# A Fourier-mixing kernel on one core: the last block of the hidden DFT matrix and its mirrors fetched by one gather of 128 half rows, blocks counted from row 1

## The chip, the cores and the metric

The kernel runs on one core of one Trainium2 chip. The metric is the device time of one execution in microseconds. Three executions of the kernel before took 199.15, 200.08 and 200.59 us; the median, 200.08 us, is its time.

## The reference

The input `x` has 2048 tokens of 576 numbers. The reference normalises each token, transforms the result with a discrete Fourier transform along the hidden dimension and one along the sequence, keeps the real part and adds the input:

```
a = einsum("bsd,ed->bse", ln(x), dft_hid_re);  b = einsum("bsd,ed->bse", ln(x), dft_hid_im)
y = einsum("ts,bse->bte", dft_seq_re, a) - einsum("ts,bse->bte", dft_seq_im, b)
h = x + y
r = ln(h) @ w_r;  idx = argmax(r)                  # one token of 2048
f = (silu(ln(h)[idx] @ w_gate) * (ln(h)[idx] @ w_up)) @ w_down      # 576 -> 4608 -> 576
out = h + ln(h);  out[idx] += f * sigmoid(r[idx])
```

The DFT matrices are inputs: the kernel must compute with what it is given, whatever it holds. Two of 2048x2048 (here `ct`, cosine and sine in turn) and two of 576x576 (here `wt`: row e holds the 576 real parts and then the 576 imaginary parts, 4608 bytes in all).

## The kernel before

**The folds and their checks.** A DFT matrix is symmetric to itself mirrored: of `wt`, row 576-e has the real part of row e and the negative of its imaginary part, and the same holds of the columns. So the kernel multiplies by half of the rows and columns and gets the other half by sums and differences. It may do so only if the matrices that it was given have these symmetries, so it checks them on the way: it loads a block and its mirror, VectorE (DVE) writes their difference into a buffer `Q` (two halves, used in turn), and ScalarE (ACT) squares that with an accumulated sum (L368) into a column of `DS`. Near the end the sums are tested; a sum that is too large sends the kernel into a generic branch. Checks of `ct` are DVE lines L375 (a half against its mirror), L380 (a block against another) and L387; those of `wt` are `off_w` (L422 to L427).

**W.** The hidden DFT matrix lies in tile `W` as three blocks: A holds rows 0 to 127, B rows 128 to 255, C rows 256 to 288. In C the real parts lie on partitions 0 to 32, and the imaginary parts of rows 256 to 287 a second time on partitions 64 to 95, so that one matmul can take both. `load_w` issues these loads on the queue of the sync engine (SP): L403 for A, B and for C's 33 rows, L405 for the 32 half rows. The mirrored rows of A, B and C are fetched row by row on GpSimd's (POOL's) queue by indirect DMAs (`gather`, L301) with row numbers from the columns of `iw`; they land in buffers of the ring R or in D and exist only for the check. `wrap_w` (ACT, L415) copies column 0 behind column 575. The matmuls with W (the hidden transform, L610) come in five steps: A and B with their real parts, with their imaginary parts, and C.

**Stages.** (1) Tokens are loaded, folded and normalised (to about 33 us); XF holds the folded tokens. (2) Sequence transform (PE, L565): halves of `ct` in two groups, `GROUPS`, each a cosine and a sine half, loaded from SP (L357) and, mirrored, gathered from POOL (L301), into the tiles D and the seven buffers of the ring R. DVE and ACT combine the results into `Z` (L579, L583). (3) Hidden transform (L610, 58.7 to 126 us), the residual sum on DVE (L619), the router's dot product (L623, L630). (4) The router's argmax, the chosen token, and the feed-forward of that token: 4608 columns of `w_gate` and `w_up` and rows of `w_down`, 31.85 MB, are loaded into places that the earlier stages leave free (R, D, XF, W, Z, Q; L1181). Their products with the token are made on POOL (L1209), DVE (L1198) and PE (L1236), their sums on ACT (L1214). (5) The last PE products (`pd`), a sum `orow` (L1249), the output.

**The order.** A planner (class `Plan`) is given every step with an engine, an estimated duration and its predecessors, and writes out each engine's order by list scheduling. It also hands out buffers (`ring`, for R and D; `qs`, for Q), and picks the order and the places of the feed-forward's weights. Every engine executes its order strictly in turn, with semaphore waits at single instructions. The wish list for stage 2 is a string: `"sffsffwsss"`, where `s` is the check of a sine block of the second group, `f` a first step of a cosine block, and `w` the check of W (`w_check`: three gathers and three `off_w`).

Of the kernel before, what the change touches and what calls it, by code (L numbers as in the profile page):

```python
# [142 lines left out]
def kernel(  # L143
# [265 lines left out]

# [3 lines left out]
    def wrap_w(n):  # L413

        act.activation(W[n][:, :, D : D + 1], W[n][:, :, 0:1], AF.Copy)  # L415

    def off_w(n, u):

        ps = W_ROWS[n]
        t, o = WM["ABC"[n]][0:ps], Q[0:ps, u % 2]  # L420
        re, im = W["ABC"[n]][0:ps, 0, :], W["ABC"[n]][0:ps, 1, :]
        dve.tensor_tensor(o[:, 0:D], t[:, 0:D], re[:, 0:D], op=OP.subtract)  # L422
# [1 line left out]
        o = o[:, 2 * D : 3 * D]
        dve.tensor_tensor(o[:, 0:287], re[:, 1:HD], re[:, D - 1 : HD : -1], op=OP.subtract)
        dve.tensor_tensor(o[:, 287:575], im[:, 1 : HD + 1], im[:, D - 1 : HD - 1 : -1], op=OP.add)
        dve.tensor_copy(o[:, 575:576], im[:, 0:1])  # L427

    W_ROWS = (P, P, 33)

# [108 lines left out]
    def folded(k, part):  # L539
        n = POS[k]  # L540
        q = FOLDED.index(k)
        e, o = FO[k] if k in PAIRS else (UF[k][:, 1:289], UF[k][:, 289:D])
        b = BE[:, n : n + 1] if k in PAIRS else BX[:, n : n + 1]
        sc = 1.0 if k in PAIRS else RX[:, n : n + 1]
        if part == 0:
            act.activation(XF[:, q, E0 + 1 : E0 + 289], e[:, :288], AF.Identity, bias=b, scale=sc)
        else:
            dve.tensor_scalar(XF[:, q, O0 + 1 : O0 + 288], o[:, :287], sc, None, op0=OP.mult)

# [138 lines left out]

    dve.memset(XF[:, :, 289 : O0 + 1], 0.0)
    dve.memset(XF[:, :, O0 + 288 : XF_W], 0.0)  # L690
    dve.memset(W["C"], 0.0)

# [170 lines left out]

    WS, WL, WRAP = [], [], []

    def w_first():
        for n in range(3):
            LAST["SP"], d = load(
                "SP", then(load_w, None, n), (0.59, 0.59, 0.22)[n], LAST["SP"], users["W" + "ABC"[n]]
            )  # L870
            WL.append(d)

    def w_check():
        for n in range(3):
# [87 lines left out]
    for j in GROUPS[0][:3]:
        c_check(j, 0)
    w_first()
    for j in GROUPS[0][3:]:
# [546 lines left out]
```

## Time and profile before

| | us |
|---|---|
| median of 3 runs | 200.08 (199.15 to 200.59) |
| profiled execution | 199.06 |
| its span | 197.1 |
| DVE busy | 166.4 (84%) |
| ACT busy | 140.5 (71%) |
| PE busy | 130.2 (66%) |
| POOL busy | 111.8 (57%) |
| moved by DMA | 77.81 MB, mean 395 GB/s |

The profiled execution took 2 us more than its span, which starts with its first and ends with its last recorded instruction. Times in a timeline count from the start of the span. A row of a timeline has the start, the duration, the engine, the line, the operation, the tile written `<-` the tiles read, and in square brackets how long the engine had stood idle before and what released it. A row of the windows has, for each engine, its busy time in that stretch (with the count of instructions), then the granted clock of TensorE, the mean busy share of the 16 DMA engines (which can come out above 1, as packets overlap) and the GB/s that they moved. "SPq" is SP's queue: its waits are those of the loads that it issues.

### The profile page before, as it was taken

How to read it: one execution, taken by the hardware profiler on the slowest of the kernel's cores; microseconds unless marked ns; L12 is line 12 of the kernel's file. 1: busy time of each engine (PE TensorE's matmuls, PEld its weight loads, DVE VectorE, ACT ScalarE, POOL GpSimd, SP SyncE). 2: the span in 40 equal slices, each digit the busy share in tenths (PEclk: the TensorE clock that was granted, in tenths of full speed). 3: DMA queues.
4: the chain of work that ended last, by engine and by line, in shares of the span. 5: the costliest groups of instructions: out<-in, count | busy, mean ns of one | idle time of the engine just before them, and what ended most of it. 6: DMA issues, size and time to landing. Idle time of an engine off the chain costs nothing. (4 is left out here: it accounts for less than half of the span.)

```text
span 197.1 us, 2789 instructions
## 1 busy us (share of the span) xinstructions
PE 130.2 (66%) x758; PEld 89.5 (45%) x758; DVE 166.4 (84%) x419; ACT 140.5 (71%) x259; POOL 111.8 (57%) x134
## 2 busy tenths in 40 slices
PE   0007889999999999999999986700241317074940
PEld 0004667755667788676866764400121103032330
DVE  4399999989899699995999999999839999987620
ACT  3298865781997879797588599989527999787600
POOL 6588888724447882398830000004556999999700
PEclk9999999999999999999999999985555555567596
DMA  5999999999999999999999999999999999999980
GB/s 183 422 412 413 409 415 406 411 394 326 401 406 396 406 379 410 409 406 415 407 408 416 422 425 419 428 421 409 430 429 417 432 423 425 423 424 421 419 354 24
DMA packets 14491, 77.81 MB, mean 395 GB/s; under 512 B 1855, under 2 KB 1859, under 8 KB 11143
## 3 DMA queue, kind: packets, MB, share of 16 engines
q1 hardware_dynamic: 10461, 56.56, 71.1%
q0 software_dynamic: 4000, 21.03, 26.5%
q8 instruction: 7, 0.11, 0.2%
q14 instruction: 13, 0.11, 0.1%
q10 hardware_dynamic: 10, 0.00, 0.0%
HBM read 72.86 MB, written 6.49 MB: 403 GB/s over the span
## 5 line engine op out<-in xcount | busy, mean ns | idle before, releaser
L368 ACT ACTIVATE Q<-Q 128x2944 bf16<-128x2944 bf16 (+5 forms) x26 | 55.4, 2132 | 15.7 <-DVE Q L380 8.2
L610 PE MATMUL py<-W,Z 128*128 128x289 f32 x180 | 45.3, 409 | 2.5 <-DVE X L619 2.5
L565 PE MATMUL ps<-D,XF 128*128 128x320 f32 (+3 forms) x216 | 44.8, 408 | 0.4 <-DMA D<-in_ct_dram 0.4
L610 PEld LDWEIGHTS py<-W,Z 128*128 128x128 f32 x180 | 33.6, 189 | 13.9 <-issue 2.2
L301 POOL DMA_INDIRECT R<-in_ct_dram,ic x21 | 29.3, 1396 | 18.0 <-DVE Q L375 14.1
L565 PEld LDWEIGHTS ps<-D,XF 128*128 128x128 f32 (+1 forms) x216 | 32.1, 172 | 12.8 <-issue 2.4
L1209 POOL TENSOR_TENSOR D<-D,Z 128x1152 f32<-128x1152 f32 x8 | 20.9, 2640 | 0.0
L667 POOL DMA_DIRECT2D out_dram<-X x1 | 0.6, 606 | 33.5 <-ACT X L661 33.5
L301 POOL DMA_INDIRECT D<-in_ct_dram,ic x11 | 14.8, 1346 | 7.6 <-DMA R<-in_ct_dram,ic 4.6
L498 ACT ACTIVATE junk<-X,XT 128x576 bf16<-128x576 f32 x16 | 12.3, 772 | 7.6 <-DVE W L459 6.4
L1214 ACT ACTIVATE junk<-D 128x576 bf16<-128x576 f32 x20 | 13.7, 683 | 3.2 <-POOL D L1209 1.6
L375 DVE TENSOR_TENSOR Q<-R,D 128x896 bf16<-128x896 f32 x11 | 11.9, 1084 | 3.9 <-DMA D<-in_ct_dram 2.4
L1236 PE MATMUL pd<-XF,H 128*1 128x144 f32 x80 | 5.3, 438 | 14.8 <-DVE H L1228 11.3
L537 PE MATMUL fo<-W,diag 128*128 128x288 f32 (+1 forms) x8 | 3.7, 640 | 16.0 <-DVE diag L528 16.0
L380 DVE TENSOR_TENSOR Q<-R,D 128x1152 bf16<-128x1152 f32 x10 | 13.4, 1348 | 0.0
L630 ACT ACTIVATE junk<-X,TD 128x576 bf16<-128x576 f32 x16 | 12.3, 766 | 1.4 <-DVE X L619 1.3
L661 ACT ACTIVATE X<-X,BB,UP 128x576 f32<-128x576 f32 x14 | 10.8, 854 | 3.1 <-DVE BB L642 3.1
L387 DVE TENSOR_TENSOR Q<-D 128x640 bf16<-128x640 f32 (+3 forms) x20 | 12.8, 694 | 0.0
L623 DVE SCALAR_TENSOR_TENSOR junk<-X,wr 128x576 bf16<-128x576 f32 x16 | 12.1, 755 | 0.3
L375 DVE TENSOR_TENSOR Q<-D 128x896 bf16<-128x896 f32 x11 | 11.8, 1082 | 0.0
L619 DVE SCALAR_TENSOR_TENSOR X<-py,X 128x576 f32<-128x576 f32 x16 | 11.6, 748 | 0.0
L375 DVE TENSOR_TENSOR Q<-R 128x896 bf16<-128x896 f32 x10 | 10.7, 1083 | 0.2 <-DMA R<-in_ct_dram,ic 0.2
(202 smaller groups left out, 257.5 us busy)
## 6 DMA issues: line engine op xcount, KB each, us to landing
D<-in_ct_dram SPq DMA_DIRECT2D x22, 576.0 KB
R<-in_ct_dram SPq DMA_DIRECT2D x10, 576.0 KB
D<-in_wu_dram SPq DMA_DIRECT2D x5, 1152.0 KB
D<-in_wd_dram SPq DMA_DIRECT2D x4, 1152.0 KB
R<-in_wg_dram SPq DMA_DIRECT2D x3, 1152.0 KB
D<-in_wg_dram SPq DMA_DIRECT2D x3, 1152.0 KB
out_dram<-X SPq DMA_DIRECT2D x2, 1440.0 KB
X<-in_x_dram SPq DMA_DIRECT2D x4, 576.0 KB
```

What stands on the lines that cost most here:

```text
L301: pool.indirect_dma_start(tile, None, view, bass.IndirectOffsetOnAxis(ap=rows, axis=0), element_offset=at)
L368: act.activation(t, t, AF.Square, accum_out=DS[0 : t.shape[0], n : n + 1])
L375: dve.tensor_tensor(o, C[j, i, True][:, 0:7, :], C[j, i, False][:, 7:0:-1, :], op=SIGN[i])
L380: dve.tensor_tensor(o, C[NK - j, i, False], C[j, i, False][:, :, ::-1], op=SIGN[i])
L387: dve.tensor_tensor(o[:, :, k::2, :], t[:, :, k::2, 0:HM], t[:, :, k::2, HM:P], op=op)
L498: act.activation(junk[:, 0:D], X[:, k, 0:D], AF.Square, bias=XT[:, n : n + 1], scale=-float(D), accum_out=VX[:, n : n + 1],)
L565: pe.matmul(cm(ZP[g, n][k % 2][p0 : p0 + m], w), XF[:, q, m0 : m0 + m], DT[g, i][:, :, k, 0:HM], start=k in (0, 1), stop=k in (6, 7),)
L610: pe.matmul(YP[GROUPS[g][c]][:, h, 0:w], Z[:, a, c * P : (c + 1) * P], w_block(a)[:, h * HD : h * HD + w], start=(a == 0), stop=(a == 4),)
L623: dve.scalar_tensor_tensor(junk2, X[:, k, 0:D], 1.0, wr, op0=OP.mult, op1=OP.mult, accum_out=TD[:, n, 0:1])
L630: act.activation(junk[:, 0:D], X[:, k, 0:D], AF.Square, bias=TD[:, n, 1:2], scale=-float(D), accum_out=VAR[:, n : n + 1],)
L1209: pool.tensor_tensor(t, t, xs.unsqueeze(1).to_broadcast([P, JW, D]), op=OP.mult)
L1214: act.activation(junk[:, 0:D], WB[w, j][:, r, :], AF.Copy, accum_out=acc[:, j + r : j + r + 1])
```

## The change

Blocks of W now start at row 1: A holds rows 1 to 128, B rows 129 to 256, and C rows 257 to 288. C is no longer loaded from SP: one gather on POOL's queue fetches 128 half rows of 2304 bytes (`wh`, `wt` seen as 1152 half rows). Partitions 0 to 31 get the real parts of rows 257 to 288, 32 to 63 those of the mirror rows 319 down to 289 and of row 0, and 64 to 127 the imaginary parts likewise (with row 288 once more in the last lane). Two half rows, the imaginary parts of rows 0 and 288, come from SP into partitions 0 and 1 behind it. So C brings its mirrors along, and `w_check` gathers mirrors for A and B only.

The half rows' numbers stand in column 2 of `iw`. They are made by a new function, `last_block_rows`: four IOTAs of 32 rows, and for the lane of row 0 a comparison, a cast, a product and a write back. This and the gather form the step `wc_first`, which is planned with the loads of W, ahead of the fourth check of the first group.

C's check, `off_wc`, writes 865 columns on 128 partitions rather than 1728 on 33: a clearing of 576 columns of Q, two differences of 31 rows, a copy of the two half rows and the column check on 64 rows (`off_e`); ACT squares 865 columns on 128 rows. The clearing of tile C at the start (L691, DVE) is gone, since the gather fills every partition. The wish list is now `"sffsffswcss"`: the mirrors of A and B are gathered and checked behind one more sine check, and `c` is C's check. The columns of XF are laid out to fit (E1 = 0, the column of row 0 at 319, O1 = 320).

```diff
@@ E0, O0, XF_W
-E0, O0, XF_W = 0, 320, 640
+E1, E_0, O1, XF_W = 0, 319, 320, 640
+D1 = 2 * P + 1
@@ index tables
+    wh = wt.rearrange("d (c e) -> (d c) e", c=2)
...
-        pool.iota(iw, pattern=[[-P, 3]], base=D, channel_multiplier=-1)
-        pool.memset(iw[0:1, 0:1], 0)
+        pool.iota(iw[:, 0:2], pattern=[[-P, 2]], base=D - 1, channel_multiplier=-1)
...
+    def last_block_rows():
+        for c in range(2):
+            p = 64 * c
+            pool.iota(iw[p : p + 32, 2:3], pattern=[[0, 1]], base=2 * D1 + c, channel_multiplier=2)
+            pool.iota(iw[p + 32 : p + 64, 2:3], pattern=[[0, 1]], base=2 * (D - D1) + c, channel_multiplier=-2)
+        r, f = iw[32:64, 2:3], [small.tile([P, 1], F32, tag=f"rw{n}", name=f"rw{n}", bufs=1)[32:64] for n in range(2)]
+        pool.tensor_scalar(f[0], r, D + 0.5, None, op0=OP.is_ge)
+        pool.tensor_copy(f[1], r)
+        pool.tensor_tensor(f[0], f[0], f[1], op=OP.mult)
+        pool.tensor_scalar(r, f[0], 1.0, 0.0, op0=OP.mult, op1=OP.add)
@@ load_w
-        name = "ABC"[n % 3]
-        if n < 3:
-            t = W[name][:, :, 0:D]
-            rows = wt[n * P : n * P + (P if n < 2 else 33), :].rearrange("p (c e) -> p c e", c=2)
-            sp.dma_start(t if n < 2 else t[0:33], rows)
-            if n == 2:
-                sp.dma_start(W[name][64:96, 0, 0:D], wt[2 * P : HD, D : 2 * D])
-            return
-        t = WM[name] = raw(b, f"w{name}m").rearrange("p a e -> p (a e)")
-        gather(t if n < 5 else t[0:33, :], wt, iw[:, n - 3 : n - 2] if n < 5 else iw[0:33, 2:3])
+        if n < 2:
+            rows = wt[n * P + 1 : (n + 1) * P + 1, :].rearrange("p (c e) -> p c e", c=2)
+            sp.dma_start(W["AB"[n]][:, :, 0:D], rows)
+        elif n == 2:
+            sp.dma_start(W["C"][0:2, 1, 0:D], wh[1 : D + 2 : D, :])
+        elif n < 5:
+            name = "AB"[n - 3]
+            t = WM[name] = raw(b, f"w{name}m").rearrange("p a e -> p (a e)")
+            gather(t, wt, iw[:, n - 3 : n - 2])
+        else:
+            gather(W["C"][:, 0, 0:D], wh, iw[:, 2:3])
@@ checks
+    def off_wc(u):
+        c, o = W["C"][:, 0, :], Q[:, u % 2, 0 : D + 289]
+        dve.memset(o[:, 0:D], 0.0)
+        for p, op in ((0, OP.subtract), (64, OP.add)):
+            dve.tensor_tensor(o[p : p + 31, 0:D], c[p + 32 : p + 63, 0:D], c[p : p + 31, 0:D], op=op)
+        dve.tensor_copy(o[32:34, 0:D], W["C"][0:2, 1, 0:D])
+        off_e(o[:, D:], c[0:64], c[64:P])
@@ plan
+    def wc_first():
+        r = LAST["POOL"] = add("POOL", 1.5, last_block_rows, LAST["POOL"])
+        LAST["POOL"], d = load("POOL", then(load_w, None, 5), 0.295, r)
+        WC.append(d)
...
+    def wc_check():
+        q, w = qs.take()
+        WS.append(add("DVE", 2.6, then(off_wc, q), WL[2], WC, w))
+        squares(q, D + 289, WS[-1])
...
-    for step in "sffsffwsss":
+    for step in "sffsffswcss":
```

What the planner makes of it is seen in the order of three engines. On POOL, the first rows are the gathers of mirrored halves of `ct` into R and D around 32 to 40 us of the profile before:

```order
L521 TENSOR_TENSOR XF<-V_111 128x2
L301 DMA R<-in_ct_dram,ic 128x896
L301 DMA D<-in_ct_dram,ic 128x896 x2
L301 DMA R<-in_ct_dram,ic 128x896 x7
L301 DMA R<-in_wt_dram,iw 128x1152
L301 DMA D<-in_wt_dram,iw 128x1152
L301 DMA D<-in_wt_dram,iw 33x1152
```

The same place now, with the semaphores that each instruction waits for (those whose names begin with DMASW are raised by the landing of POOL's own DMAs; `rw` are the two small tiles of `last_block_rows`):

```order
L315 DMA R<-in_ct_dram,ic 128x896
L315 DMA D<-in_ct_dram,ic 128x896 [waits PE_49]
L235 IOTA iw 32x1
L236 IOTA iw 32x1 [waits Pool_49]
L235 IOTA iw 32x1
L236 IOTA iw 32x1 [waits Pool_49]
L238 TENSOR_SCALAR rw_403<-iw 32x1 [waits DMASW5_49,DMASW4_49,DMASW6_49,DMASW1_49,DMASW7_49,DMASW0_49,Pool_49]
L239 CAST rw_404<-iw 32x1
L240 TENSOR_TENSOR rw_403<-rw_403,rw_404 32x1 [waits Pool_49]
L241 TENSOR_SCALAR iw<-rw_403 32x1 [waits Pool_49]
L315 DMA W<-in_wt_dram,iw 128x576 [waits Pool_49]
L315 DMA D<-in_ct_dram,ic 128x896 [waits PE_49]
```

Eight small instructions and C's gather have moved in between the two gathers into D; the first of the four that reshape the numbers waits for six of POOL's DMA semaphores. Behind the last row stand eight gathers into R, one into D and the two of W's mirrors.

On SP, the loads of the halves of `ct` and of W, before:

```order
L357 DMA D<-in_ct_dram 128x1152 x10
L357 DMA R<-in_ct_dram 128x1152 x2
L357 DMA D<-in_ct_dram 128x1152
L403 DMA W<-in_wt_dram 128x2x576 x2
L403 DMA W<-in_wt_dram 33x2x576
L405 DMA W<-in_wt_dram 32x576
L357 DMA D<-in_ct_dram 128x1152
```

and now:

```order
L371 DMA D<-in_ct_dram 128x1152 x10
L371 DMA R<-in_ct_dram 128x1152 x2
L371 DMA D<-in_ct_dram 128x1152
L415 DMA W<-in_wt_dram 128x2x576 x2
L417 DMA W<-in_wt_dram 2x576
L371 DMA D<-in_ct_dram 128x1152
```

Two narrow loads have become one of two half rows at the same place. Further down SP's order, the first of the feed-forward's weights goes into XF, where before it went into R.

On DVE, the checks of C and what stands around them, before (`py` is a result of the hidden transform, `TD` the router's dot products):

```order
L427 CAST Q<-W 128x1
L422 TENSOR_TENSOR Q<-D,W 33x576
L423 TENSOR_TENSOR Q<-D,W 33x576
L425 TENSOR_TENSOR Q<-W 33x287
L426 TENSOR_TENSOR Q<-W 33x288
L427 CAST Q<-W 33x1
L619 SCALAR_TENSOR_TENSOR X,TD<-py_1_551,X 128x576
```

and now:

```order
L446 CAST Q<-W 128x1
L451 MEMSET Q 128x288
L453 TENSOR_TENSOR Q<-W 31x576 x2
L454 CAST Q<-W 2x576
L443 TENSOR_TENSOR Q<-W 64x287
L445 TENSOR_TENSOR Q<-W 64x288
L446 CAST Q<-W 64x1
L649 SCALAR_TENSOR_TENSOR junk_124,TD<-X,wr 128x576
```

Seven instructions stand where five stood, and they read no mirror buffer. The first check of W, which before stood ahead of the first two residual sums (L619), now stands behind them and three more checks of `ct`.

More of the change, by code (lines that the diff above doesn't have):

```diff
@@ L232, in unit_matrix @@
         dve.scalar_tensor_tensor(
-            sgn, ident[:, D // 2 - 2 * P : D // 2 - 2 * P + 1], -0.5, pm1, op0=OP.mult, op1=OP.add
+            sgn, ident[:, HD - D1 : HD - D1 + 1], -0.5, pm1, op0=OP.mult, op1=OP.add
         )
@@ L413, in wrap_w, with off_e @@
     def wrap_w(n):
-        act.activation(W[n][:, :, D : D + 1], W[n][:, :, 0:1], AF.Copy)
+        c = 1 if n == "C" else 2
+        act.activation(W[n][:, 0:c, D : D + 1], W[n][:, 0:c, 0:1], AF.Copy)
     def off_w(n, u):
-        ps = W_ROWS[n]
-        t, o = WM["ABC"[n]][0:ps], Q[0:ps, u % 2]
-        re, im = W["ABC"[n]][0:ps, 0, :], W["ABC"[n]][0:ps, 1, :]
+        t, o = WM["AB"[n]], Q[:, u % 2]
+        re, im = W["AB"[n]][:, 0, :], W["AB"[n]][:, 1, :]
         dve.tensor_tensor(o[:, 0:D], t[:, 0:D], re[:, 0:D], op=OP.subtract)
         dve.tensor_tensor(o[:, D : 2 * D], t[:, D : 2 * D], im[:, 0:D], op=OP.add)
[L424 to L429, printed above, removed]
+        off_e(o[:, 2 * D : 3 * D], re, im)
+    def off_e(o, re, im):
+        h = o.shape[-1] - 289 if re.shape[0] == P else 0
+        dve.tensor_tensor(o[0 : re.shape[0], 0:287], re[:, 1:HD], re[:, D - 1 : HD : -1], op=OP.subtract)
+        o = o[:, h:] if h else o[64:P]
+        dve.tensor_tensor(o[:, 0:288], im[:, 1 : HD + 1], im[:, D - 1 : HD - 1 : -1], op=OP.add)
+        dve.tensor_copy(o[:, 288:289], im[:, 0:1])
+    def off_wc(u):
[5 more added lines that the diff above has]
+        off_e(o[:, D:], c[0:64], c[64:P])
     VX = mp.tile([P, NK], F32, name="VX")
@@ L514, in biases @@
         q = FOLDED.index(ORDER[n0])
-        d0 = XF[:, q : q + (h if n0 < 14 else 2), E0]
+        d0 = XF[:, q : q + (h if n0 < 14 else 2), E_0]
         if n0 == 14:
@@ L545, in folded @@
         if part == 0:
[L546 removed]
+            act.activation(XF[:, q, E1 : E1 + 288], e[:, :288], AF.Identity, bias=b, scale=sc)
         else:
[L548 removed]
+            dve.tensor_scalar(XF[:, q, O1 : O1 + 287], o[:, :287], sc, None, op0=OP.mult)
     ZP = {}
@@ L559, in seq @@
         ZP[g, n] = [zbank(f"ps{g}_{n}_{h}") for h in range(2)]
-        parts = [(0, E0 + 2 * P, 64, 0), (1, O0 + 2 * P, 64, 64)]
+        parts = [(0, E1 + 2 * P, 64, 0), (1, O1 + 2 * P, 64, 64)]
         if n < 4:
-            parts = [(n // 2, (E0, O0)[n // 2] + (n % 2) * P, P, 0)]
+            parts = [(n // 2, (E1, O1)[n // 2] + (n % 2) * P, P, 0)]
         for q, k in enumerate(FOLDED):
@@ L687, in then @@
         return lambda: f(*args)
-    dve.memset(XF[:, :, 289 : O0 + 1], 0.0)
-    dve.memset(XF[:, :, O0 + 288 : XF_W], 0.0)
-    dve.memset(W["C"], 0.0)
+    dve.memset(XF[:, :, E1 + 288 : E_0], 0.0)
+    dve.memset(XF[:, :, O1 + 287 : XF_W], 0.0)
     moved = [add("DMA", 1.5, None)]
@@ L862, in c_check @@
         squares(u, QW if j in PAIRS else 7 * P, n)
-    WS, WL, WRAP = [], [], []
+    WS, WL, WRAP, WC = [], [], [], []
     def w_first():
@@ L868, in w_first @@
             LAST["SP"], d = load(
-                "SP", then(load_w, None, n), (0.59, 0.59, 0.22)[n], LAST["SP"], users["W" + "ABC"[n]]
+                "SP", then(load_w, None, n), (0.59, 0.59, 0.005)[n], LAST["SP"], users["W" + "ABC"[n]]
             )
             WL.append(d)
+    def wc_first():
+        r = LAST["POOL"] = add("POOL", 1.5, last_block_rows, LAST["POOL"])
+        LAST["POOL"], d = load("POOL", then(load_w, None, 5), 0.295, r)
+        WC.append(d)
     def w_check():
-        for n in range(3):
-            u, d = ring("POOL", load_w, (0.59, 0.59, 0.16)[n], n + 3)
+        for n in range(2):
+            u, d = ring("POOL", load_w, 0.59, n + 3)
             q, w = qs.take()
@@ L961 @@
         c_half(0, c, m)
[L962 to L965, printed above, removed]
+    for n, j in enumerate(GROUPS[0]):
+        if n == 3:
+            w_first()
+        if n == 3:
+            wc_first()
         c_check(j, 0)
@@ L976 @@
     for n in range(3):
-        WRAP.append(add("ACT", 0.25, then(wrap_w, "ABC"[n]), WL[n], SEQ[0, 2][0]))
+        WRAP.append(add("ACT", 0.25, then(wrap_w, "ABC"[n]), WL[n] if n < 2 else WC, SEQ[0, 2][0]))
     no_more("D2")
@@ L985 @@
             c_first(1, 0, (next(first),))
+        elif step == "c":
+            wc_check()
         else:
```

2 lines of the change are left out of this document (1 added, 1 removed).

## The prediction

> **What bounds the kernel now.** I read the page first (busy shares, the slices of DMA, the chain), then the last rows of PE and POOL, then DVE's waits going back, and last the stretch of DMA in which W's last block is loaded.
>
> Busy shares of the engines, and DMA in 40 slices of 4.9 us:
>
> ```profile
> PE 130.2 (66%) x758; PEld 89.5 (45%) x758; DVE 166.4 (84%) x419; ACT 140.5 (71%) x259; POOL 111.8 (57%) x134
> DMA  5999999999999999999999999999999999999980
> GB/s 183 422 412 413 409 415 406 411 394 326 401 406 396 406 379 410 409 406 415 407 408 416 422 425 419 428 421 409 430 429 417 432 423 425 423 424 421 419 354 24
> ```
>
> The transfers are busy from 4.9 us to about 190 at some 410 to 430 GB/s. No engine is as full. The end, on PE, and the start and the last row of POOL's products:
>
> ```profile
> 188.02 1.16 PE L1236 MATMUL pd<-D,H 128*1 128x144 f32 x32 [0.74 <-DVE hs L1227]
> 190.11 1.16 PE L1236 MATMUL pd<-W,H 128*1 128x144 f32 x32 [0.93 <-SPq L1339]
> 149.47 2.62 POOL L1209 TENSOR_TENSOR XF<-XF,Z 128x1152 f32<-128x1152 f32 x1 [2.96 <-ACT Z L1084]
> 183.09 2.64 POOL L1209 TENSOR_TENSOR D<-D,Z 128x1152 f32<-128x1152 f32 x1
> ```
>
> The last product waits 0.93 us for its weights, so the end is DMA's. Right behind stands a chain of compute: POOL's products, one after another from 149.47 to 185.73, and their sums. If all transfers came earlier, the end would come earlier by 0.93 us, and by more only if 149.47 does so too. That start hangs on the chosen token, hence on DVE. Its waits in the stages that the change touches:
>
> ```profile
> 42.88 1.09 DVE L375 TENSOR_TENSOR Q<-R,D 128x896 bf16<-128x896 f32 x1 [0.52 <-ACT Q L368]
> 52.18 1.09 DVE L375 TENSOR_TENSOR Q<-R,D 128x896 bf16<-128x896 f32 x1 [0.95 <-ACT Q L368]
> 66.17 1.09 DVE L375 TENSOR_TENSOR Q<-R 128x896 bf16<-128x896 f32 x1 [0.22 <-DMA R<-in_ct_dram,ic]
> 69.07 0.76 DVE L422 TENSOR_TENSOR Q<-R,W 128x576 bf16<-128x576 f32 x1 [1.80 <-DMA R<-in_wt_dram,iw]
> 93.52 1.09 DVE L375 TENSOR_TENSOR Q<-R,D 128x896 bf16<-128x896 f32 x1 [2.41 <-DMA D<-in_ct_dram]
> ```
>
> Up to 60 us DVE waits for ACT alone; later it waits for DMA, 0.22 + 1.80 + 2.41 = 4.43 us in all. So before 60 DVE and ACT set the pace, and after it DMA does. On this the sum rests.
>
> **C's narrow loads.** Two loads on SP bring C, 148.5 and 72 KB, onto 33 and 32 partitions. When they move, DMA dips (windows of 1 and 2 us; the last two columns are DMA's busy share and GB/s):
>
> ```profile
> 44.00:45.00 1.00, 1.00 (x10) 0.57 (x8) 1.00 (x1) 0.31 (x1) 0.00 (x0) 1.00 1.09 423
> 45.00:46.00 1.00, 1.00 (x12) 0.50 (x9) 1.00 (x2) 0.00 (x0) 0.00 (x0) 1.00 0.97 348
> 46.00:47.00 1.00, 1.00 (x10) 0.51 (x8) 1.00 (x2) 0.00 (x0) 0.49 (x1) 1.00 1.11 266
> 47.00:48.00 1.00, 1.00 (x7) 0.44 (x4) 1.00 (x4) 0.16 (x1) 1.00 (x1) 1.00 1.02 281
> 48.00:49.00 1.00, 1.00 (x5) 0.74 (x4) 1.00 (x2) 0.37 (x1) 0.70 (x2) 1.00 1.02 318
> 49.00:50.00 1.00, 1.00 (x5) 0.68 (x5) 1.00 (x2) 0.60 (x1) 1.00 (x1) 1.00 1.01 358
> 58.00:59.00 1.00, 1.00 (x5) 0.55 (x4) 1.00 (x2) 0.91 (x4) 1.00 (x1) 1.00 1.10 412
> 59.00:60.00 1.00, 1.00 (x5) 0.76 (x4) 1.00 (x4) 0.97 (x4) 0.69 (x2) 1.00 0.81 326
> 70.00:72.00 2.00, 2.00 (x11) 1.77 (x10) 2.00 (x7) 0.71 (x3) 1.70 (x2) 1.00 1.05 350
> ```
>
> From 45 to 50 the engines of DMA are full, but move 348 + 266 + 281 + 318 + 358 = 1571 KB where 412 GB/s would make 2060: 489 KB, or 489/412 = 1.2 us, are lost. Likewise the gather of C's 33 mirror rows, at 70 to 72: 2 x (412 - 350) = 124 KB, 0.3 us. A gather of 128 half rows on all partitions has the shape of the other gathers, beside which there is no such dip, so I take both losses as gone; if the half rows (2304 bytes, half as long as the rows of the other gathers of W) are slow too, some of the 1.2 us comes back.
>
> The Trainium skill bears on this dip: "SBUF — State Buffer", section "Door 1: The DMA port swizzle", says that bandwidth goes by how many of 16 ports the partitions of a transfer reach, and by its table partitions 0 to 31 or 64 to 95 alone reach 8. At half rate, 220.5 KB would cost an extra 0.54 us (my estimate by that page); the dip shows 1.2, so the direction agrees and the size does not.
>
> But what is 1.2 us of DMA at 45 to 50 worth? Where the loads of that stretch wait:
>
> ```profile
> SPq L357 <- DVE Q L375: 24.1, 9, 5.3
> 46.51 1.55 POOL L301 DMA_INDIRECT R<-in_ct_dram,ic  x1 [5.69 <-DVE Q L375]
> 57.82 1.81 POOL L301 DMA_INDIRECT R<-in_ct_dram,ic  x1 [2.73 <-DVE Q L375]
> 59.94 0.94 POOL L301 DMA_INDIRECT R<-in_wt_dram,iw  x1 [0.30 <-DVE Z L583]
> ```
>
> SP waits 24.1 us for checks on DVE to free a buffer, and POOL 5.69 and 2.73 us in this stretch. DVE itself does not wait for DMA there. So a faster DMA at 45 to 50 runs out of loads sooner: already in the window 59:60 its share falls to 0.81 and 326 GB/s, that is, the queues are nearly dry. I take the 1.2 us as lost again to idle DMA: **0, bounds -1.2 to 0**. C's bytes there grow from 220.5 KB to 297 (128 + 2 half rows), 0.17 us, with the same cover.
>
> After 60, where DMA sets the pace, the 148.5 KB of the mirror gather are gone, 148.5/412 = 0.36 us, and its dip of 0.3: **-0.66, bounds -0.66 to 0** (0 if the queues stay dry there).
>
> **POOL's wait.** The order has a new wait: on POOL the instruction that reshapes the row numbers stands until POOL's own gathers have landed, that of D issued just before it among them. POOL's rows there now:
>
> ```profile
> 34.02 1.61 POOL L301 DMA_INDIRECT D<-in_ct_dram,ic  x1 [0.31 <-issue]
> 35.93 1.02 POOL L301 DMA_INDIRECT D<-in_ct_dram,ic  x1 [0.30 <-issue]
> 38.00 1.55 POOL L301 DMA_INDIRECT R<-in_ct_dram,ic  x1 [1.05 <-DVE Q L375]
> 39.86 0.97 POOL L301 DMA_INDIRECT R<-in_ct_dram,ic  x1 [0.30 <-issue]
> ```
>
> How long from issue to landing? The gather of 57.82 feeds the DVE row of 66.17, 8.35 us, that of 59.94 the row of 69.07, 9.13 us. So the one of 34.02 lands at 42.4 to 43.2. Four small instructions follow; the nearest rows are POOL's on one element:
>
> ```profile
> 143.28 0.25 POOL L1048 TENSOR_SCALAR near<-cit 1x1 f32<-1x1 int32 x1 [1.29 <-DVE cit L1023]
> 144.78 0.18 POOL L1054 TENSOR_SCALAR late<-near 1x1 int32<-1x1 f32 x1
> ```
>
> These are the first and the last of seven, 1.68 us, 0.24 each: 1.0 us for four. Then C's gather (0.94 to 1.6 us with 0.3 between): queued behind it, the gathers of 35.93, 38.00 and 39.86 start at about 45.0, 46.3 and 47.6, 8 to 9 us late. That of 46.51 was idle 5.69 us before, so by about 50 POOL has caught up. Two things hang on this. First, DMA: SP's loads alone can't fill it while POOL is silent from 36 to 44; three gathers of 459 KB (128 x 896 x 4) come later. Some of that hole is the idleness that DVE's pace causes anyway, some pushes bytes to the other side of 60: **+0.5, bounds 0 to +2.0** (from nothing to two gathers, 2 x 459/412 = 2.2). Second, DVE: the check at 52.18 reads the gather of 38.00. Issued at 46.3, it lands at 48.6 if the queues are empty (1.2 us of issue, 1.1 of bytes) and at 54.7 with the 8.35 us of a full queue; the middle is 51.6. Since SP's loads are then ahead of their buffers and the queue is short, I take it as in time: **0, bounds 0 to +2.5** (54.7 - 52.18).
>
> The Trainium skill speaks against moving C from SP to POOL: "SBUF — State Buffer", the box on "The "DVE blocks DMA" trap (SWDGE)" in "SBUF: two separate sides", says that a DMA issued from GpSimd can starve while DVE holds the shared port. The rows above show gathers of 0.94 to 1.81 us with DVE busy, no long starvation; by that rule alone the one gather added would cost at most the spread of these rows, 0.9 us on POOL (an estimate), and I add nothing for it.
>
> **The checks of W.** C's check before, on DVE, first and last row, and its square on ACT:
>
> ```profile
> 74.71 0.74 DVE L422 TENSOR_TENSOR Q<-D,W 33x576 bf16<-33x576 f32 x1
> 76.78 0.14 DVE L427 CAST Q<-W 33x1 bf16<-33x1 f32 x1
> 76.95 1.64 ACT L368 ACTIVATE Q<-Q 33x1728 bf16<-33x1728 bf16 x1
> 1.75 0.30 DVE L690 MEMSET XF<- 128x288 f32 x1
> ```
>
> It took 76.92 - 74.71 = 2.21 us. The new one has the same two differences and column checks, plus a clearing of 576 bf16 columns, as many bytes as the 0.30 us row, and a copy of 576 (between 0.14, the one-column row, and 0.74): +0.4 to +1.0, say +0.6 us, against 4.43 us of waits for DMA behind 60: nothing; if that cover were gone, +0.6. ACT's square is half as wide, 1.64 x 865/1728 = 0.8, so -0.8 us where ACT isn't waited for. The clearing of C at the start goes; DVE waited for POOL's iota there, so nothing. The mirrors of A and B, behind one more check, come later, and the residual sums earlier: their cover is the same 4.43 us. The first weights now wait for XF rather than R, which PE's sequence transform reads to 103.8; until then POOL's last gathers and SP's last halves are in the queues, so nothing, or up to 1 us of idle DMA if they run out.
>
> **The sum.** 0 - 0.66 + 0.5 + 0 + 0 = -0.16 us: 198.9 beside the profiled 199.06, which is 1.0 below the median. On the median, 200.08 - 0.2 = **199.9 us**.
>
> **Rivals.** (B) *The dip's gain reaches the end.* For it: DMA is busy in all slices and the end waits for DMA. Against it: the dry window at 59. Then -1.2 - 0.66 + 0.17 = -1.7 us: 198.4; 149.47 comes down with it, since the 4.43 us of waits for DMA are on its way. Without it, -0.93 is the most: 199.15.
>
> (C) *POOL's wait for its own gather makes DVE late.* The place is the check at 52.18; it decides once the gather that was at 38.00 lands after that, which is an issue-to-landing time above 5.9 us (52.18 - 46.3), where full queues took 8.35. Against it: the queue is short there. What DVE loses there passes on: its order is solid from there to 60 and frees the buffers of all later loads. With DMA's hole at the middle of its bounds, +1.0, and the 0.66 gained, a landing half way, at 53.4, costs 1.25 + 1.0 - 0.66 = +1.6, the latest one 2.5 + 1.0 - 0.66 = +2.8; the middle is +2.2: **202.3**.
>
> (D) *Half rows are no faster, and the wait is covered:* nothing changes but 0.07 MB of 77.81: 200.0.
>
> **Chances.** My forecast 0.48, B 0.27, C 0.2, D 0.05. The range takes in B with half of the spread of the three runs (0.7) below it, 198.4 - 0.7 = 197.7, and of C the nearer half, to 202.3. A change of over 1%, 2.0 us, is about what a measurement of this kernel can tell from none. Faster by that (under 198.08): four tenths of B, 0.11, and 0.04 of my forecast, for the places of the feed-forward's weights that the planner chose anew. Slower (over 202.08): half of C, 0.10, and 0.05 of my forecast for the same. Between them 0.70.
>
> **What would show it.** In the profile after: no windows under 330 GB/s at full share around 45 to 50 (else the half rows are slow); POOL idle some 7 us or more ahead of its small instructions, released by a DMA into D, at about 42 to 43; its next gather of `ct` at about 45; DVE's check near 52 released by ACT (mine) or by a DMA into R (C); a dry window at 55 to 60 deeper than 0.81 (mine) or none (B); the last product still released by SP's queue, by under 1 us. The forecast is wrong if DVE passes 60 us at a different time by over 1 us.

## The result and the profile after

The changed kernel takes 202.12 us in the median of 20 runs, the kernel before 199.79 us beside it. The ratio is 1.0129, with a 95% interval of 1.0106 to 1.0152: slower by 1.3%, some 2.6 us. The forecast was 199.9, in a range of 197.7 to 202.3 that just holds the time. The profiled execution took 202.28 us, with a span of 200.5. (All ratios here are formed of undisturbed executions alone, so a ratio can differ from the quotient of two medians; ratios are what I compare.)

The page after, engines, DMA in slices and its total:

```profile
PE 130.9 (65%) x758; PEld 90.4 (45%) x758; DVE 166.7 (83%) x420; ACT 139.9 (70%) x259; POOL 112.1 (56%) x141
DMA  6999999995899999999999999999999999999990
GB/s 188 419 414 409 413 411 408 404 402 162 260 412 405 410 410 412 405 407 416 404 410 385 421 425 428 419 413 429 396 429 422 426 426 430 421 428 407 414 380 27
DMA packets 14530, 77.73 MB, mean 388 GB/s; under 512 B 1831, under 2 KB 1835, under 8 KB 11310
```

Busy times have hardly moved. DMA has a hole: the tenth and eleventh slices (45 to 55 us) moved 162 and 260 GB/s, where before (44 to 54 us) they moved 326 and 401. What made it stands on POOL, around C's gather:

```profile
33.45 0.97 POOL L315 DMA_INDIRECT D<-in_ct_dram,ic  x1 [0.30 <-PE fo L563]
...
41.00 1.57 POOL L238 TENSOR_SCALAR rw<-iw 32x1 f32<-32x1 int32 x1 [5.86 <-issue]
42.61 0.18 POOL L239 CAST rw<-iw 32x1 f32<-32x1 int32 x1
42.87 0.18 POOL L240 TENSOR_TENSOR rw<-rw,rw 32x1 f32<-32x1 f32 x1
43.14 1.04 POOL L241 TENSOR_SCALAR iw<-rw 32x1 int32<-32x1 f32 x1
44.46 1.87 POOL L315 DMA_INDIRECT W<-in_wt_dram,iw  x1 [0.27 <-POOL iw L241]
46.64 1.39 POOL L315 DMA_INDIRECT D<-in_ct_dram,ic  x1 [0.30 <-issue]
48.33 1.97 POOL L315 DMA_INDIRECT R<-in_ct_dram,ic  x1 [0.30 <-DVE Q L389]
```

POOL stands 5.86 us until its gather of 33.45 has landed (the row names no releaser; the instruction waits for the landings of six of POOL's DMAs, and this gather is the last issued of them). Then it spends 3.2 us on four small instructions (41.00 to 44.18) and 2.2 on C's gather, and it issues at 48.33 the gather that DVE's check near 52 us reads; before, that one was issued at 38.00. DVE then:

```profile
43.05 1.09 DVE L389 TENSOR_TENSOR Q<-R,D 128x896 bf16<-128x896 f32 x1 [0.52 <-ACT Q L382]
55.85 1.09 DVE L389 TENSOR_TENSOR Q<-R,D 128x896 bf16<-128x896 f32 x1 [4.45 <-ACT W L431]
74.59 1.36 DVE L394 TENSOR_TENSOR Q<-D 128x1152 bf16<-128x1152 f32 x1 [1.90 <-DMA D<-in_ct_dram]
```

The check that started at 52.18 starts at 55.85. The row names ACT's copy of a column of W as the releaser. That can't be it: the check doesn't read W, and it is the mirror just gathered into R that it waits for; in a run below without POOL's wait, the same check starts at 52.39, before that copy (at 55.2 in both). Of the 4.45 us, 0.95 were waited for ACT before too; 3.5 us are new.

The windows of DMA in the stretch, after and then before (4 us each; the last two columns are DMA's share and GB/s):

```profile
44.00:48.00 4.00, 4.00 (x31) 2.00 (x28) 4.00 (x6) 0.48 (x3) 3.42 (x3) 1.00 0.60 212
48.00:52.00 4.00, 4.00 (x16) 2.81 (x17) 3.40 (x5) 2.96 (x2) 3.39 (x3) 1.00 0.76 183
52.00:56.00 4.00, 4.00 (x17) 2.81 (x15) 0.15 (x1) 3.56 (x8) 3.04 (x4) 1.00 0.92 328
```

```profile
44.00:48.00 4.00, 4.00 (x29) 2.02 (x26) 4.00 (x6) 0.47 (x2) 1.49 (x1) 1.00 1.05 329
48.00:52.00 4.00, 4.00 (x16) 2.85 (x15) 3.23 (x5) 2.97 (x3) 2.77 (x3) 1.00 1.02 371
52.00:56.00 4.00, 4.00 (x16) 2.83 (x15) 3.82 (x4) 3.75 (x9) 1.55 (x1) 1.00 1.01 409
```

In these 12 us the changed kernel moved 4 x (212 + 183 + 328) = 2892 KB, the kernel before 4 x (329 + 371 + 409) = 4436 KB. The difference, 1544 KB, is 3.75 us at 412 GB/s. DVE's 3.5 us and DMA's 3.75 us are not to be added: the run without the wait, below, gains 1.7% (3.3 us) in all. Little of it is given back behind, for DMA is nearly full to the end, and the last product still waits for its weights:

```profile
152.74 2.63 POOL L1247 TENSOR_TENSOR XF<-XF,Z 128x1152 f32<-128x1152 f32 x1 [3.05 <-DMA D<-in_wu_dram]
193.12 1.16 PE L1274 MATMUL pd<-Z,H 128*1 128x144 f32 x32 [0.83 <-SPq L1377]
```

POOL's products start 3.27 us later than before (149.47), and the last product 3.01 us later (190.11).

There is a second difference, which the hole mostly hides. SP's last loads of halves of `ct` and its first weights, after and then before:

```profile
96.33 1.33 SPq L371 DMA_DIRECT2D R<-in_ct_dram  x2
106.33 0.33 SPq L1219 DMA_DIRECT2D XF<-in_wg_dram  x1
```

```profile
82.57 8.89 SPq L357 DMA_DIRECT2D R<-in_ct_dram  x3
99.84 0.33 SPq L1181 DMA_DIRECT2D R<-in_wg_dram  x1
102.05 0.33 SPq L1181 DMA_DIRECT2D XF<-in_wu_dram  x1
```

The first weights go to XF, and SP waits for the sequence transform on PE to have read it; they start 6.5 us later than before. Not all of that is the new place: in the run below that has the same hole but the old place, they start at 103.20, which leaves 3.1 us to it. C's mirror gather was one of the steps that took a buffer of the ring. Without it every later step takes the next buffer earlier in the ring, which moves one of SP's last loads into R behind five loads into D and the last two behind one more, and leaves another buffer first for the weights.

### The profile page after: what moved, and what is told of

Read it like the earlier page. It is cut to its first block, busy times and chain, and to the rows that moved or that the text cites. A ratio compares the mean times of both kernels' runs of the same rounds, so it can differ in the third digit from the quotient of the medians.

```text
span 200.5 us, 2785 instructions
## 1 busy us (share of the span) xinstructions
PE 130.9 (65%) x758; PEld 90.4 (45%) x758; DVE 166.7 (83%) x420; ACT 139.9 (70%) x259; POOL 112.1 (56%) x141
## 5 line engine op out<-in xcount | busy, mean ns | idle before, releaser
L382 ACT ACTIVATE Q<-Q 128x2944 bf16<-128x2944 bf16 (+5 forms) x26 | 54.8, 2106 | 17.0 <-DVE Q L394 8.1
L315 POOL DMA_INDIRECT R<-in_ct_dram,ic x23 | 27.9, 1211 | 18.6 <-DVE Q L389 13.2
L389 DVE TENSOR_TENSOR Q<-R,D 128x896 bf16<-128x896 f32 x17 | 18.3, 1084 | 5.0 <-ACT W L431 4.5
L1247 POOL TENSOR_TENSOR D<-D,Z 128x1152 f32<-128x1152 f32 x7 | 18.2, 2628 | 0.0
L315 POOL DMA_INDIRECT D<-in_ct_dram,ic x9 | 10.9, 1207 | 3.8 <-issue 1.8
L1252 ACT ACTIVATE junk<-D 128x576 bf16<-128x576 f32 x16 | 10.9, 683 | 2.8 <-POOL D L1247 2.3
L1274 PE MATMUL pd<-D,H 128*1 128x144 f32 x96 | 6.3, 441 | 9.7 <-DVE H L1266 9.5
L394 DVE TENSOR_TENSOR Q<-R,D 128x1152 bf16<-128x1152 f32 x9 | 12.2, 1352 | 0.0
L269 PE MATMUL pmt<-ident,gt 128*128 128x128 f32 x4 | 1.2, 454 | 15.6 <-DVE gt L274 15.6
L563 PEld LDWEIGHTS fo<-W,diag 128*128 128x128 f32 x8 | 2.5, 331 | 17.0 <-DVE diag L554 16.2
```

Of the source, the lines that this page charges most:

```text
L315: pool.indirect_dma_start(tile, None, view, bass.IndirectOffsetOnAxis(ap=rows, axis=0), element_offset=at)
L382: act.activation(t, t, AF.Square, accum_out=DS[0 : t.shape[0], n : n + 1])
L389: dve.tensor_tensor(o, C[j, i, True][:, 0:7, :], C[j, i, False][:, 7:0:-1, :], op=SIGN[i])
L394: dve.tensor_tensor(o, C[NK - j, i, False], C[j, i, False][:, :, ::-1], op=SIGN[i])
L1247: pool.tensor_tensor(t, t, xs.unsqueeze(1).to_broadcast([P, JW, D]), op=OP.mult)
```

## The experiments

Three theories were tried first: the wait on POOL makes the whole loss, and the narrow loads were covered (1); the same, but the narrow loads' dip reaches the end (2); the loss comes from the rest (3).

**The row numbers without a wait on POOL.** The IOTAs move to the other index tables, the four small instructions to DVE; the order of all else is that of the changed kernel, but for one gather that moves past a POOL instruction early on and two pairs of DVE instructions that change places near the end.

```diff
+            LAST["POOL"] = o = add("POOL", 0.5, last_block_rows, LAST["POOL"])
+            ROWS = add("DVE", 0.4, last_block_fix, o)
...
-        r = LAST["POOL"] = add("POOL", 1.5, last_block_rows, LAST["POOL"])
-        LAST["POOL"], d = load("POOL", then(load_w, None, 5), 0.295, r)
+        LAST["POOL"], d = load("POOL", then(load_w, None, 5), 0.295, LAST["POOL"], ROWS)
```

> The changed kernel, with the row numbers of the last block made early: the four IOTAs on POOL with the other index tables, the four small instructions that reshape them on DVE, so that nothing on POOL waits for a gather to land. All else, the gather of the last block and its place in the order among them, stays. Theory 1 (the wait of 5.9 us on POOL, ahead of the gathers, makes the whole loss, and the narrow loads' dip was covered by idle DMA): the hole in DMA at 44 to 56 us goes, DVE starts its check near 52 us in time, and the time is that of the kernel before less 0.66 us (the mirrors of the last block): about 199.1. Theory 2 (the wait makes the loss, and the dip's 1.2 us reach the end too): about 198.1. Theory 3 (the loss comes from the rest: the gather in POOL's queue, the half rows, the changed places of the feed-forward's weights): about 202, as the changed kernel.

Measured: ratio to before 0.9964 (0.9922 to 1.0006). The wait is worth 1.0129 / 0.9964 = 1.7%, give or take 0.5 by the two intervals, more than the whole loss. Its DVE timeline has the check back in its place, and its windows show where the rest of the gain is lost:

```profile
52.39 1.09 DVE L391 TENSOR_TENSOR Q<-R,D 128x896 bf16<-128x896 f32 x1 [0.96 <-ACT Q L384]
73.06 1.36 DVE L396 TENSOR_TENSOR Q<-D 128x1152 bf16<-128x1152 f32 x1 [4.54 <-DMA D<-in_ct_dram]
```

```profile
52.00:56.00 4.00, 4.00 (x16) 2.84 (x15) 3.61 (x4) 3.75 (x9) 1.80 (x2) 1.00 0.97 307
92.00:96.00 4.00, 4.00 (x18) 3.22 (x17) 4.00 (x6) 3.18 (x3) 2.58 (x3) 1.00 0.96 352
96.00:100.00 4.00, 4.00 (x20) 3.53 (x19) 4.00 (x6) 2.75 (x3) 3.09 (x4) 1.00 0.94 308
100.00:104.00 4.00, 4.00 (x26) 3.02 (x26) 4.00 (x9) 3.71 (x8) 2.84 (x2) 1.00 1.01 387
104.00:108.00 4.00, 4.00 (x33) 2.60 (x30) 4.00 (x8) 3.97 (x5) 0.00 (x0) 1.00 0.92 355
108.00:112.00 4.00, 4.00 (x18) 3.12 (x17) 3.84 (x7) 2.98 (x8) 0.00 (x0) 1.00 0.94 350
```

From 92 to 112 DMA moved 4 x 1752 = 7.0 MB where 412 GB/s would make 8.2: 3.0 us short. That is the second difference, no longer hidden. (The profiled execution took 200.53 us, some 1.3 us more than the ratio stands for, so the shortage may be less in others.)

**The wait alone, in the kernel before.** The eight instructions are inserted at the same place, into a column that nobody reads.

```diff
+    LAST["POOL"] = add("POOL", 0.0, last_block_rows, LAST["POOL"])
     for j in GROUPS[0][3:]:
```

> The kernel before, with the eight instructions that make the row numbers inserted on POOL at the place where the change has them, into a column that nobody reads; order and loads are else those of the kernel before, word for word. Theory 1 and 2: POOL stands there some 6 us, the gathers behind it start 7 to 9 us late, DVE waits 2 to 3.5 us near 52 us, and the time is that of before plus 2 to 3 us: 202 to 203. Theory 3: within 0.5 us of before, 199.8.

Measured: 1.0104 (1.0063 to 1.0145), some 2.1 us, at the lower end of what theory 1 gave. POOL stood 6.82 us:

```profile
41.96 0.26 POOL L237 TENSOR_SCALAR rw<-iv 32x1 f32<-32x1 int32 x1 [6.82 <-issue]
```

No C gather stands behind it here, so the next gather starts at 44.19 instead of 46.64. So the gather that DVE's check near 52 us reads starts at 46.37 instead of 48.33, the check is in time, and DVE's stall comes at the check two gathers later:

```profile
46.37 1.59 POOL L314 DMA_INDIRECT R<-in_ct_dram,ic  x1 [0.30 <-DVE Q L388]
52.08 1.09 DVE L388 TENSOR_TENSOR Q<-R,D 128x896 bf16<-128x896 f32 x1 [0.95 <-ACT Q L381]
59.00 1.09 DVE L388 TENSOR_TENSOR Q<-R 128x896 bf16<-128x896 f32 x1 [2.49 <-DMA R<-in_ct_dram,ic]
```

The gather of 46.37 landed in at most 5.7 us. Theory 3 is out as the whole cause: the wait costs by itself.

**A shorter wait.** The same eight instructions in the changed kernel, planned ahead of the third check rather than the fourth.

```diff
+        if n == 2:
+            LAST["POOL"] = add("POOL", 1.5, last_block_rows, LAST["POOL"])
         if n == 3:
             w_first()
```

> The changed kernel, with the same eight instructions on POOL one place further up, ahead of the third check's two gathers. POOL then waits for a gather that was issued 5 us earlier: by the landing times of the traces to about 33.5 us, a stand of some 1 to 2 us in place of 5.9, and 3 us of small instructions. Theory 1: most of the loss goes, since the gathers are late by 3 to 4 us instead of 8 to 10: 199.5 to 200.5. Theory 2: 198.5 to 199.5. Theory 3: 202.

Measured: 0.9989 (0.9944 to 1.0033). POOL stands 1.18 us instead of 5.86:

```profile
33.76 0.49 POOL L238 TENSOR_SCALAR rw<-iw 32x1 f32<-32x1 int32 x1 [1.18 <-DMA R<-in_ct_dram,ic]
```

So it is the length of the stand that costs, not that the instructions are on POOL: with 4.7 us less of it the ratio falls by 1.4%, and what is left, 0.25% above the run with none, is within the intervals.

**The old wish list.** As the run with the row numbers on DVE, with the checks of W back at their old place.

```diff
-    for step in "sffsffswcss":
+    for step in "sffsffwcsss":
```

> As the run with the row numbers on DVE, and the mirrors of A and B and all checks of W back at the place of the kernel before in the wish list ("sffsffwcsss"), which also gives the feed-forward's last weights the places that they have in the kernel before. Theories 1 and 2: the place of the checks of W matters little: within 0.5 us of the run with the row numbers on DVE. Theory 3, in so far as the later checks or the feed-forward's places make the loss: 1 to 2 us faster than that run.

Measured: 1.0036 (0.9995 to 1.0078), 0.7% behind the run without this edit. I had expected no difference, or a gain by theory 3; the later place of W's checks helps, if anything (the two intervals overlap a little). The first weights go to XF here too: I had said that the feed-forward gets back its old places, and only the last ones do. That led to the theory of the ring.

**The ring turned back.** C's check puts the first free buffer to the end of the list, as if C's mirrors still took it. With the old wish list this gives SP, but for the loads of W, the order of the kernel before.

```diff
     def wc_check():
+        free.append(free.pop(0))
         q, w = qs.take()
```

> As the run with the row numbers on DVE and the old wish list, and in C's check the first free buffer of the ring is put to the end of the ring unused, as if C's mirrors still took one. With that, SP's order (but for the loads of W) and the feed-forward's places are those of the kernel before. Theory R (new: leaving out C's mirror gather turns the ring by one buffer, so that SP's last loads of a half into R stand behind five loads into D and wait for DVE, and the first weights go to XF, which PE reads to 107 us; DMA runs short at 92 to 112 us, by 3.0 us in the trace of the run with the row numbers on DVE): this removes it. With theory 1 on the narrow loads (their dip was covered) the time is 0.66 us under before, 199.2; with theory 2 1.7 us under it, 198.2. If the ring is of no account: as the run without it, 0.4% above before, 200.6.

Measured: 0.9946 (0.9912 to 0.9981), and once more, beside the last run below:

> The same kernel as the run of the old wish list with the ring turned back, beside the next one on one chip. As then 0.5% under before, 198.7.

0.9963 (0.9931 to 0.9994). Against 1.0036, turning the ring back is worth 0.7 to 0.9%, each give or take 0.5. The edit does more than turn the ring: the planner also orders the later work of DVE and ACT anew around the other buffers, in this run and in the other runs with the ring turned back. The ratios are those of the edit as a whole; that it acts by SP's loads and the first weights is read from the windows of DMA.

The same edit in the changed kernel, with its wait on POOL:

> The changed kernel with the ring turned back by one buffer in C's check, and nothing else: POOL's wait of 5.9 us stays. If the wait alone carries the loss (theory 1; the shortage behind 92 us is covered there, since DMA is 3 us late anyway: its windows at 92 to 112 lack 0.4 us): as the changed kernel, 1.3% above before, or 0.4 us less, 202.0 to 202.4. If the ring carries the loss: about 199.5 to 200.

Measured: 1.0084 (1.0059 to 1.0108), 0.45% under the changed kernel, give or take 0.34. I had expected at most 0.2%, since the hole would cover it; the interval doesn't exclude that. And with both, the changed kernel's own wish list, no wait and the ring turned back:

> The changed kernel with its own wish list, the row numbers on DVE (no wait on POOL) and the ring turned back by one buffer: the fourth corner of wait and ring. Theory W+R (the wait and the turned ring are the two causes; each costs less where the other one stands, since both show as DMA running short): faster than before by 0.5 to 0.9%, as the run with the old wish list, 198.0 to 198.9, and without the windows under 400 GB/s at 92 to 112 us that the run with the turned ring has. If the later place of W's checks costs by itself: 199.5 or more.

Measured: 0.9923 (0.9893 to 0.9953), 198.37 us in the median: faster than both kernels, and the shortage at 92 to 112 us is all but gone (I had expected no window under 400 GB/s; one has 387, and the two behind those shown have 417 and 428):

```profile
92.00:96.00 4.00, 4.00 (x19) 3.39 (x18) 3.69 (x6) 2.84 (x3) 3.09 (x4) 1.00 1.00 387
96.00:100.00 4.00, 4.00 (x20) 3.51 (x20) 4.00 (x6) 3.02 (x3) 3.09 (x4) 1.00 1.03 400
100.00:104.00 4.00, 4.00 (x35) 2.60 (x35) 3.87 (x9) 3.17 (x4) 0.56 (x1) 1.00 1.02 406
```

This closes a square, ratios to the kernel before:

| | ring as changed | ring turned back |
|---|---|---|
| wait on POOL | 1.0129 | 1.0084 |
| no wait | 0.9964 | 0.9923 |

The wait costs 1.7% in the one column and 1.6% in the other, each give or take 0.4 to 0.5; both are clear. The ring costs 0.45% with the wait (give or take 0.34) and 0.4% without it (give or take 0.52, so by this row alone it could be nothing; the pair with the old wish list is the one that shows it without the wait). I had expected twice that the two would cover each other: the ratios show no sign of it, but the intervals would hide a part. What is left of the change without these two is a gain of 0.77% (0.5 to 1.1%), 1.5 us.

**The kernel before without C's mirrors, and with the ring turned back.** `w_check` runs over A and B alone, so C isn't checked; the second run adds the line that turns the ring at the end of `w_check`.

```diff
-        for n in range(3):
+        for n in range(2):
```

> The kernel before without the gather of C's mirrors and without C's check (this part of the test of the inputs is left out). The ring has one taker less and turns as in the changed kernel: the first weights go to XF. Theory R: the shortage at 92 to 112 us, 1 to 3 us, against 0.66 us saved for the mirrors and 2.2 us of DVE: 200 to 202. If the ring is of no account: 199.2 or less.

> As the run without C's mirrors and check, with the ring turned back by one buffer, so that SP's order and the first places of the weights are those of the kernel before. It shows what the mirror gather is worth by itself: 0.66 us under before, 199.2 (0.36 for the bytes, 0.3 for the dip); theory R: 1 to 2 us under the run without it.

Measured: 1.0276 (1.0229 to 1.0323) and 1.0052 (1.0013 to 1.0091). Turning the ring back is worth 2.2% here, more than expected. But with the ring turned back, what should have been a gain of 0.66 us is still a loss of 1.0 (0.3 to 1.8): less work made the kernel slower. In the first of the two, DVE, without C's check, comes sooner to a check whose load is late, and PE waits for DVE:

```profile
96.28 1.36 DVE L380 TENSOR_TENSOR Q<-R,D 128x1152 bf16<-128x1152 f32 x1 [7.41 <-DMA R<-in_ct_dram]
```

```profile
92.91 4.12 PE L565 MATMUL ps<-D,XF 128*128 128x256 f32 x18 [0.78 <-DMA D<-in_ct_dram]
98.36 1.13 PE L565 MATMUL ps<-D,XF 128*128 128x256 f32 x4 [1.33 <-DVE Z L583]
102.29 10.07 PE L565 MATMUL ps<-D,XF 128*128 128x256 f32 x50 [2.80 <-DVE Z L583]
```

```profile
100.00:104.00 4.00, 1.71 (x4) 1.44 (x5) 4.00 (x6) 2.81 (x3) 3.39 (x3) 0.63 0.72 228
104.00:108.00 4.00, 4.00 (x11) 3.11 (x10) 4.00 (x9) 4.00 (x7) 0.06 (x1) 0.52 0.57 203
108.00:112.00 4.00, 4.00 (x38) 2.50 (x36) 4.00 (x6) 2.92 (x7) 0.00 (x0) 1.00 0.26 46
```

In the kernel before:

```profile
92.10 12.04 PE L565 MATMUL ps<-D,XF 128*128 128x256 f32 x72 [0.42 <-DMA D<-in_ct_dram]
```

In the third pause the granted clock fell (0.63 and 0.52 in the first two windows, the third column from the right; in windows of 1 us it is 1.00 at 100, 0.53 at 101 and 0.50 from 102 to 107). With the pauses and the low clock the transform ended at 112.36 instead of 104.14; XF, where the first weights go, came free only about then, and DMA stood at 46 GB/s. The one profile of the second run has nearly the same pauses (1.18, 1.32 and 2.81 us, behind a wait of DVE of 7.80 us), but its first weights go to R and start at 103.16, not at 110.26; it is of an execution of 202.72 us, longer than most of its run (median 201.20), and so says little of the others. These runs agree with the theory of the ring, then, but why leaving out C's check makes the kernel slower even with the ring turned back stays open. They don't give a price for the mirror gather, which stays unmeasured by itself.

**Narrow loads added.** In the kernel with the old wish list and both repairs, four loads of 30 or 32 half rows are put behind C's two.

```diff
             sp.dma_start(W["C"][0:2, 1, 0:D], wh[1 : D + 2 : D, :])
+            for p in (2, 32, 64, 96):
+                q = p + 30 if p == 2 else p + 32
+                sp.dma_start(W["C"][p:q, 1, 0:D], wt[p : q, 0:D])
```

> The kernel beside it, and behind C's two half rows four more loads of 30 or 32 half rows each onto the partitions 2 to 31, 32 to 63, 64 to 95 and 96 to 127 of a part of W that nobody reads, 290 KB, 1.3 times what the kernel before loads narrow. Theory 1 (the dip of narrow loads near 46 to 50 us is covered, since the checks on DVE hold back the loads there): the dip comes back in the windows, DMA is less dry behind it, and the time stays within 0.5 us of the kernel beside it. Theory 2 (what is lost there reaches the end): 1.2 x 1.3 = 1.6 us for the dip and 0.7 us for the bytes later, 201.

Measured: 0.9989 (0.9970 to 1.0007), against 0.9963 beside it and 0.9946 in the earlier series: 0.5 to 0.9 us more, with intervals that overlap. The dip is back:

```profile
46.00:47.00 1.00, 1.00 (x10) 0.50 (x8) 1.00 (x2) 0.00 (x0) 0.49 (x1) 1.00 1.09 402
47.00:48.00 1.00, 1.00 (x7) 0.44 (x4) 1.00 (x4) 0.16 (x1) 1.00 (x1) 1.00 1.09 208
48.00:49.00 1.00, 1.00 (x5) 0.75 (x4) 1.00 (x2) 0.37 (x1) 0.69 (x2) 1.00 1.06 251
49.00:50.00 1.00, 1.00 (x5) 0.68 (x5) 1.00 (x2) 0.60 (x1) 1.00 (x1) 1.00 1.01 332
```

So the dip comes with these loads of some 32 rows each. Whether it is for the few partitions that each one reaches or for the few rows no run here separates; the four of them together reach nearly all partitions. Most of what the dip loses is covered: 0.5 to 0.9 us is far from the 2.3 of theory 2, and the bytes alone would be 0.7 us. Whether it stays within the 0.5 us of theory 1 the intervals don't tell.

## Why the prediction was wrong

The range held the time, and the sign was wrong: a small gain was forecast, and a loss of 1.3% came. By the prediction's own steps:

- **What bounds the kernel** held. DMA is full to the end, the last product waits for it by under 1 us (0.83), and POOL's products move with DVE.
- **POOL's wait was seen, with its place and its reason, and mis-sized in the sum. This is the step that failed.** The landing that POOL waits for came at 41.0, 1.4 us earlier than said. But the four small instructions took 3.2 us instead of 1.0, C's gather 2.2 with its gap instead of 1.2 to 1.9, and the gather into D behind it 1.7 instead of 1.3. So the gather that was at 38.00 started at 48.33, not 46.3. It was in use 7.5 us later, where the middle that I took allowed 5.3 (46.3 to 51.6). Of the 4.2 us from 51.6 to 55.85, 2.0 are the later start and 2.2 the longer landing. The run with the wait alone bears this out: there the same gather started at 46.37, nearly as I had said, landed in at most 5.7 us, and the check was in time. In the changed kernel DVE lost 3.5 us where I took 0 and bounded by 2.5, and DMA's hole was 3.75 us where I took 0.5 and bounded by 2.0 (two gathers, by the prediction's own division, are 2.2). In the time the wait is worth 3.3 us, where the sum has 0.5.
- **Rival C** is what happened, mechanism and place; it was given a chance of 0.2 and 202.3 us. The argument against it ("the queue is short there") was true, DMA's share was 0.76, and it didn't decide: from a start at 48.33 even the 5.3 us of the middle give 53.6, past 52.18. That C's 202.3 lies so near the measured 202.12 is partly luck: its sum has 1.0 us for the hole, knows nothing of the ring's 0.9, and has 0.66 for a gain of 1.5.
- **The first weights in XF** were priced at nothing, or up to 1 us if SP's and POOL's queues ran out. They ran out (3.0 us short at 92 to 112 us in the run with the row numbers on DVE). The price of the turned ring, of which this place is a part, is 0.45% (0.9 us) in the changed kernel and 0.4 to 0.9% without the wait. I had named the new place of the weights and not asked why it had changed: leaving out C's mirror turns the ring of buffers, which also moves a load of `ct` into R behind five loads into D (83.19 in the changed kernel). That showed in SP's order, and I hadn't read it.
- **C's narrow loads**, 0 of 1.2 us, were right in kind. Without them DMA runs dry sooner, at 52 to 56 (307 GB/s in the run with the row numbers on DVE), and adding more of them costs little. (C's bytes come to 292.5 KB, 130 half rows in the unit of the 220.5, and not 297; the price stays 0.17 us.)
- **The gain of C's mirrors, 0.66 us, and rival B.** The change without wait and turned ring gains 1.5 us, near B's 1.7. The sum's -0.66 accounts for less than half. Of the rest the later checks of W may have some 0.3% (0.9923 against 0.9946 and 0.9963, but the intervals overlap); the remainder is open, and a part of the dip may be in it. So B is neither shown nor ruled out.
- **The half rows** aren't slow: in the run with the row numbers on DVE, where C's gather is issued at 35.03, DMA moves 395 to 414 GB/s in all windows of 2 us from 36 to 46. **C's check** on DVE took 3.34 us (83.59 to 86.93) where I said 2.8, without effect that the runs show.
- **The signs.** POOL stood 5.9 us rather than 7; its next gather of `ct` came at 46.64 rather than 45; the check near 52 us was released by the gather into R, which was C's sign; and DVE passed 60 us 3.5 us late, which the prediction had named as the sign of being wrong.

## What to carry to other kernels

An instruction that must wait for a DMA of its own engine's queue costs more than the wait: add up what stands behind it in that queue, each at the time that it takes in the trace beside what then runs, up to the first thing that another engine needs. For the landing take the range that the trace shows, not the middle of a measured time and an estimate of the bytes; when the margin is as narrow as here (0.6 us), say that it can go either way. Put such an instruction ahead of the DMAs or on an engine with slack: here moving four 32-element instructions to DVE, and their IOTAs to the start, gave back 1.7%. And when a change drops a user of a rotating set of buffers, read what all later users get, for the order changes far behind the edit; here one `pop` and `append` was worth 0.4 to 0.9% in the changed kernel's runs.

## What the runs showed of the hardware

**Landing of a gather.** From issue to the instruction that needed it, POOL's gathers of 459 KB took 7.55 us (33.45 to 41.00) and 7.5 us (48.33 to 55.85) in the changed kernel and 8.56 us (33.40 to 41.96) in the kernel before with the wait. But there the one of 46.37 took at most 5.7 us (to 52.08), with DMA at 0.83 of its time from 46 to 48, and in the changed kernel C's gather, 295 KB issued at 44.46 when DMA was running dry (0.60 of its time from 44 to 48), landed in 4.4 us by the profile's list of DMA issues.

So the time isn't fixed, and it can be shorter when DMA has less to do; why the gather of 48.33 took 7.5 with DMA at 0.76 and 0.92 of its time the runs don't show.

**Small instructions on POOL beside DVE.** POOL's instruction of 32 elements took 0.18 us at 42.61 and 42.87, in a pause of DVE, but 1.57 at 41.00 and 1.04 at 43.14. DVE's check, started at 43.05, ended at 44.14, and POOL's at 44.18. In the kernel before with the wait the last of the four took 1.10 us, from 42.81, beside DVE's check of 42.77 (1.09 us). The Trainium skill, "SBUF — State Buffer", section "Who interferes with whom", says that a DVE instruction with two SBUF inputs contends with a GpSimd instruction that reads SBUF; the trace agrees, with POOL instructions that end with the DVE instruction beside them (44.18 and 44.14). My 0.24 us each came from POOL rows for which I hadn't looked at what DVE did.

**The clock of PE after a pause.** In the kernel before without C's mirrors PE paused for 0.78, 1.33 and 2.80 us within 10 us. In the third pause the granted clock fell to 0.50; it was back at 1.00 from 108 us, after 5.6 us of matmuls without a pause. The Trainium skill, "TensorE: Matmul & The Clock Gate", section "Part 1: The HAM clock gate", says that the clock is halved by default and that activity releases it; the trace agrees (0.50, then 1.00).
